# The 16-bit copy of thirteen weight rows goes from ScalarE to GpSimd, in a kernel of window attention and a two-layer product

## The chip, the cores and the metric

The kernel runs on one core of a Trainium2 chip. The metric is the device time of one execution in microseconds. Engines are named as in the profile: PE (TensorE, matrix products), DVE (VectorE), ACT (ScalarE), POOL (GpSimd) and SP (SyncE, which here starts the transfers). Each takes its own instructions in order and waits at an instruction until what it reads has been written and what it overwrites has been read.

## The reference

Attention over four batches, eight heads, 768 positions and a head size of 64, with four sink keys and a window of 128 keys; then a layer of 512 x 2048 with the square of the positive part, and one of 2048 x 512.

```python
scores = scale * np.matmul(q, k.transpose(0, 1, 3, 2))
keep = is_sink | in_window
scores = np.where(keep, scores, -1000000000.0)
scores = scores - np.max(scores, axis=-1, keepdims=True)
a = np.exp(scores)
a = a / (np.sum(a, axis=-1, keepdims=True) + 1e-09)
attn_out = np.matmul(a, v).astype(np.float32)
x = np.ascontiguousarray(attn_out.transpose(0, 2, 1, 3)).reshape(B * S, H * D)
h = np.maximum(x @ w_in, 0.0)
out = (h * h @ w_out).astype(np.float32)
```

The weights w_in and w_out come as 64-bit numbers and are turned into pairs of 32-bit ones on the chip.

## The kernel before

The tokens are taken in eight chunks of 384 (half a batch). A chunk has four pairs of heads; "pair" below is one pair of heads of one chunk, counted from the first. For a pair, PE makes scores (L255), DVE masks them out of PSUM and finds the largest (L263), ACT takes the exponential and the sums (L266), DVE makes the reciprocal of the sums (L279, L280), and POOL multiplies the probabilities by it (L291, three instructions for each of the two heads) and copies the sink part out (L304, L305). PE transposes the probabilities (L360), ACT and DVE copy them out of PSUM (L367, L365), PE multiplies them with the values (L408, L411), and ACT and DVE write the result as a high and a low part, x (L419, L420).

The products of the two layers go over 16 blocks of 128 hidden columns: PE makes ph (L467, 12 matmuls), ACT the squares (L478, L481, L483), DVE the low part gl (L490), PE adds the block into po (L505), which needs gh, gl and the block's row of w_out.

The weights come in 32 rows of 128 x 512 numbers, loaded as raw (L564). A row is made into a high and a low part by `split_steps`: DVE forms the high part t (L575, L577), a copy takes one 16-bit word of each number into one half of m (L579) while DVE puts other bits into the other half (L580), DVE takes the exponent eb (L582), ACT writes the high part to its place (L588), and DVE forms the low part from m and eb (L589), so L589 waits for the copy. The tile m has one buffer: the copy of a row waits for L589 of the row before. In the order of the rows, rows 0 to 3 are of w_in, 4 to 6 of w_out (wo), 7 to 10 of w_in (wi), 11 to 15 of w_out, 16 of w_in.

The first two chunks and rows 0 to 16 (`EARLY` is 17) stand in a part whose order is written out by hand for all five engines (L628 to L751): the instructions of each engine stand as the code calls them. `fill(n)` puts in n further steps of the rows, `normalise` the instructions of POOL for a pair. After that part a scheduler with priorities sets the order. The probabilities of a head have four buffers, the scores of this part two banks ("att") most of the time.

Of the kernel before, what the change touches and what calls it, by code (L numbers as in the profile page):

```python
# [37 lines left out]
def f32(ap):  # L38
    return ap.bitcast(F32)
# [3 lines left out]
def sink_window_attention_moe(  # L43
# [11 lines left out]
    nc = tc.nc  # L55
# [13 lines left out]
    with ExitStack() as fast:  # L69
# [490 lines left out]
        def load_row(n):  # L560
            if n in raws or n >= NROW:
                return
            raws[n] = wp.tile([P, WR, 2], I32, tag=f"wo{NFC - 4 + n % 4}", name=f"raw_{n}")
            nc.sync.dma_start(out=raws[n].rearrange("p w t -> p (w t)"), in_=row_of(n))  # L564

        def split_steps(n):
            kind, fq, j = order[n]
            load_row(n)
            top = raws[n][:, :, 1]
            words = raws[n].rearrange("p w t -> p (w t)").bitcast(U16).rearrange("p (w t) -> p w t", t=4)  # L570
            t1 = ap2.tile([P, WR], I32, tag="t1", name=f"t1_{n}")
            m = ap1.tile([P, WR], I32, tag="m", name=f"m_{n}")
            eb = ap1.tile([P, WR], I32, tag="eb", name=f"eb_{n}")
            m16 = m.bitcast(U16).rearrange("p (w t) -> p w t", t=2)
            nc.vector.tensor_scalar(t1, top, 3, 0x3FFFF000, op0=ALU.logical_shift_left, op1=ALU.bitwise_and)  # L575
            yield
            nc.vector.scalar_tensor_tensor(t1, top, -0x40000000, t1, op0=ALU.bitwise_and, op1=ALU.bitwise_or)  # L577
            yield
            nc.scalar.copy(m16[:, :, 0], words[:, :, 1])  # L579
            nc.vector.tensor_scalar(m16[:, :, 1], words[:, :, 2], 0x1FF, None, op0=ALU.bitwise_and)  # L580
            yield
            nc.vector.tensor_scalar(eb, t1, -0x800000, None, op0=ALU.bitwise_and)  # L582
            yield
            if kind == "i":
                row = wi[:, j, fq]
            else:
                row = wo[j] = wp.tile([P, 2, DM], F32R, tag=f"wo{j}", name=f"wo_{j}")
            nc.scalar.copy(row[:, 0, :], f32(t1))  # L588
            nc.vector.scalar_tensor_tensor(row[:, 1, :], m, 2.0**-36, f32(eb), op0=ALU.mult, op1=ALU.mult)  # L589
            load_row(n + AHEAD)  # L590

        def split_row(n):
            keep = tc.cur_priority
            tc.cur_priority = keep + (10 if n >= HALF else 0)
            for _ in split_steps(n):
                pass
            tc.cur_priority = keep + 12
# [19 lines left out]
        def row_steps():  # L617
            for n in range(NROW):
                yield from split_steps(n)
                split.append(n)  # L620
                yield
# [5 lines left out]
        EARLY = HALF + 1  # L627
# [396 lines left out]
```

## Time and profile before

| | |
|---|---|
| three runs, median | 701.47 us (700.86 to 702.70) |
| the profiled execution | span 701.0 us |
| PE busy | 685.4 us |
| DVE, ACT, POOL busy | 430.6, 438.5, 228.6 us |
| L579 on ACT | 32 copies, 24.8 us |

The span goes from the first to the last instruction of the profiled execution; the page has no other time for it. In the order in time, the first number of a row is the start in us and the second the duration in us (of all the instructions that the row merges, x3 for three), and what stands in brackets is idle time of the engine before it and what ended it. An instruction can start on an engine shortly before the one ahead ends. In the groups of one line, three durations in ns are the shortest, the median and the longest.

### The profile page before, as it was taken

How to read it: one execution, taken by the hardware profiler on the slowest of the kernel's cores; microseconds unless marked ns; L12 is line 12 of the kernel's file. 1: busy time of each engine (PE TensorE's matmuls, PEld its weight loads, DVE VectorE, ACT ScalarE, POOL GpSimd, SP SyncE). 2: the span in 40 equal slices, each digit the busy share in tenths (PEclk: the TensorE clock that was granted, in tenths of full speed). 3: DMA queues.
4: the chain of work that ended last, by engine and by line, in shares of the span. 5: the costliest groups of instructions: out<-in, count | busy, mean ns of one | idle time of the engine just before them, and what ended most of it. 6: DMA issues, size and time to landing. Idle time of an engine off the chain costs nothing.

```text
span 701.0 us, 11730 instructions
## 1 busy us (share of the span) xinstructions
PE 685.4 (98%) x3862; PEld 593.2 (85%) x3862; DVE 430.6 (61%) x1181; ACT 438.5 (63%) x1240; POOL 228.6 (33%) x433
## 2 busy tenths in 40 slices
PE   8889999999999999999999999999999999999995
PEld 4567889998888888888889888888988889889994
DVE  7989799746567666565565666666556665542221
ACT  6888877655666776676667777667676544422221
POOL 5764400034464432342343443233244242200000
PEclk9999999999999999999999999999999999999998
DMA  7476476412424323332434432243432210010001
GB/s 240 154 225 197 141 230 211 128 51 62 130 74 141 104 81 106 108 112 82 119 91 148 123 99 79 82 143 91 114 104 78 73 44 16 0 41 6 1 0 51
DMA packets 37028, 71.51 MB, mean 102 GB/s; under 512 B 4384, under 2 KB 14368, under 8 KB 36960
## 3 DMA queue, kind: packets, MB, share of 16 engines
q1 hardware_dynamic: 36816, 70.55, 34.1%
q8 instruction: 33, 0.54, 0.3%
q14 instruction: 35, 0.29, 0.1%
q10 hardware_dynamic: 144, 0.13, 0.1%
HBM read 62.80 MB, written 7.86 MB: 101 GB/s over the span
## 4 chain that ended last, share of the span: by engine, by line
PE 92%; ACT 3%; DVE 2%; POOL 2%; issue 1%; DMA 0%; SPq 0%; POOLq 0%; DVEq 0%
PE po L505 37%; PE ph L467 37%; PE xo L408 6%; PE s L259 5%; PE pt L378 2%; PE xo L411 2%; PE s L255 1%; POOL P L291 1%; ACT P L266 1%; PE pt L360 1%; DVE P L263 0%; DMA kn<-in_k_dram 0%; ACT m L579 0%; POOL PSK L304 0%; DVE t L577 0%
## 5 line engine op out<-in xcount | busy, mean ns | idle before, releaser
L467 PE MATMUL ph<-x,wi 128*128 128x384 f32 x1536 | 305.7, 340 | 0.0
L467 PEld LDWEIGHTS ph<-x,wi 128*128 128x128 f32 x1536 | 265.1, 188 | 9.1 <-issue 1.4
L505 PE MATMUL po<-wo,gh 128*128 128x512 f32 (+1 forms) x770 | 244.2, 398 | 0.0
L227 POOL TENSOR_TENSOR KS<-kn,KS 128x408 fp32r<-128x408 f32 (+1 forms) x48 | 58.4, 1217 | 317.0 <-ACT KS L226 317.0
L505 PEld LDWEIGHTS po<-wo,gh 128*128 128x128 f32 x770 | 135.9, 188 | 19.1 <-issue 1.3
L505 PE MATMUL po<-wo,gl 128*128 128x512 f32 x385 | 151.6, 394 | 0.0
L266 ACT ACTIVATE P<-P,nbs 128x264 f32<-128x264 f32 (+1 forms) x192 | 94.3, 491 | 75.7 <-DVE nbs L263 75.4
L486 DVE TENSOR_TENSOR ph<-ph,r 128x384 f32<-128x384 f32 x96 | 54.0, 562 | 76.7 <-ACT r L478 76.6
L263 DVE CUSTOM_DVE_ANT_0 P<-s,masks 128x264 f32<-128x264 f32 x160 | 67.1, 429 | 53.3 <-PE s L259 49.5
L291 POOL TENSOR_SCALAR P<-P,rs 128x136 f32<-128x136 f32 (+2 forms) x192 | 85.5, 461 | 30.1 <-DVE rs L280 23.4
L478 ACT ACTIVATE r<-ph 128x384 f32<-128x384 f32 x96 | 46.7, 487 | 77.7 <-PE ph L467 74.9
L490 DVE TENSOR_TENSOR gl<-ph,gh 128x384 fp32r<-128x384 f32 x128 | 71.0, 555 | 25.2 <-ACT ph L483 13.5
L505 PEld LDWEIGHTS po<-wo,gl 128*128 128x128 f32 x385 | 72.2, 188 | 16.0
L229 DVE TENSOR_TENSOR QS<-qn,QS 64x384 fp32r<-64x384 f32 x48 | 43.7, 910 | 25.0 <-ACT QS L228 24.6
L259 PE MATMUL s<-KS,QS 128*128 128x264 f32 (+1 forms) x288 | 56.9, 280 | 0.0
L286 POOL TENSOR_TENSOR P<-P 128x256 f32<-128x256 f32 (+1 forms) x48 | 48.1, 1001 | 26.7 <-ACT P L266 26.2
L259 PEld LDWEIGHTS s<-KS,QS 128*128 128x128 f32 x288 | 51.9, 188 | 5.0 <-DVE nbs L263 0.5
L481 ACT ACTIVATE gh<-r 128x384 fp32r<-128x384 f32 x96 | 50.2, 523 | 2.1
L384 DVE TENSOR_TENSOR PTF<-pt,halves 128x256 f32<-128x256 f32 x96 | 36.3, 418 | 21.8 <-PE pt L378 21.1
L408 PE MATMUL xo<-PTF,vn 128*64 128x256 f32 x448 | 45.9, 342 | 0.7 <-ACT PTF L367 0.7
L408 PEld LDWEIGHTS xo<-PTF,vn 128*64 128x64 f32 x448 | 31.2, 136 | 17.4 <-issue 9.3
L226 ACT CAST KS<-kn 128x408 fp32r<-128x408 f32 (+1 forms) x48 | 28.3, 589 | 26.0 <-issue 12.6
(108 smaller groups left out, 676.0 us busy)
## 6 DMA issues: line engine op xcount, KB each, us to landing
raw<-in_moe_w_in_dram SPq DMA_DIRECT2D x16, 512.0 KB, 4.5
raw<-in_moe_w_out_dram SPq DMA_DIRECT2D x16, 512.0 KB, 3.4
half<-in_moe_w_in_dram SPq DMA_DIRECT2D x32, 256.0 KB, 3.0
half<-in_moe_w_out_dram SPq DMA_DIRECT2D x32, 256.0 KB, 3.1
kn<-in_k_dram SPq DMA_DIRECT2D x24, 272.0 KB, 4.1
qn<-in_q_dram SPq DMA_DIRECT2D x32, 192.0 KB, 3.8
out_dram<-ob SPq DMA_DIRECT2D x23, 256.0 KB, 2.5
kn<-in_k_dram SPq DMA_DIRECT2D x24, 204.0 KB, 3.6
```

Source lines behind the costliest of these rows:

```text
L227: nc.gpsimd.tensor_tensor(KS[:, 1, 0:nk], st["kn"][:, hh, 0:nk], f32(KS[:, 0, 0:nk]), op=ALU.subtract)
L259: nc.tensor.matmul(ps[:, 0:n], st["QS", hh][:, qcols], flat[:, a, c0 : c0 + n], start=(a == 0), stop=(a == 1))
L263: nc.vector.tensor_tensor_reduce(Pt[:, i, 0:n], ps[:, 0:n], mask[:, 0:n], -SCALE, BIG, ALU.add, ALU.min, nb)
L266: nc.scalar.activation(Pt[:, i, 0:n], Pt[:, i, 0:n], AF.Exp, bias=nb, scale=-1.0, accum_out=sm[:, i : i + 1])
L286: nc.gpsimd.tensor_tensor(Pt[:, j0:NQ, 0:P], Pt[:, j0:NQ, 0:P], Pt[:, j0:NQ, BS:BAND], op=ALU.add)
L291: nc.gpsimd.tensor_scalar(Pt[:, j, 0:n], Pt[:, j, 0:n], rs[:, hh, j : j + 1], 1.0, op0=ALU.mult, op1=ALU.mult)
L408: nc.tensor.matmul(xo[h * D : h * D + D, cols], lhsT, rhs, start=(n == 0), stop=False, skip_group_check=True)
L467: nc.tensor.matmul(ph[:, 0:TOK], wi_at(i, cc, fc), xt[:, cc, :], start=(m == 0), stop=(m == 3 * NCC - 1),)
L481: nc.scalar.activation(gh, r, AF.Square)
L486: nc.vector.tensor_tensor(ph[:, 0:TOK], ph[:, 0:TOK], r, op=ALU.mult)
L490: late = lambda: nc.vector.tensor_tensor(gl, ph[:, 0:TOK], f32(gh), op=ALU.subtract)
L505: nc.tensor.matmul(po[t][:, e], gt[:, ts_], wo[f][:, i, e], start=(f == f0 and j == 0), stop=(f == f1 - 1 and j == 2), skip_group_check=True,)
```

## The change

One line. For rows 4 to 16 the copy is called on POOL (`nc.gpsimd.tensor_copy`) instead of ACT; rows 0 to 3 and 17 to 31 stay as they were.

```diff
             nc.vector.scalar_tensor_tensor(t1, top, -0x40000000, t1, op0=ALU.bitwise_and, op1=ALU.bitwise_or)
             yield
-            nc.scalar.copy(m16[:, :, 0], words[:, :, 1])
+            (nc.gpsimd.tensor_copy if 4 <= n < EARLY else nc.scalar.copy)(m16[:, :, 0], words[:, :, 1])
             nc.vector.tensor_scalar(m16[:, :, 1], words[:, :, 2], 0x1FF, None, op0=ALU.bitwise_and)
             yield
```

What this does to the order on POOL, at the end of the sixth pair's normalisation (P of pair index 1 in the second chunk; the last number of a name only tells tiles apart), with rows 6 to 9 added:

```order
 L304 CAST PSK_140<-P_1_1_642 128x6x8
 L305 TENSOR_TENSOR PSK_140<-P_1_1_642,PSK_140 128x3x8
+L579 COPY m_707<-raw_650 128x512
+L579 COPY m_757<-raw_690 128x512
+L579 COPY m_791<-raw_731 128x512
+L579 COPY m_845<-raw_788 128x512
 L291 TENSOR_SCALAR P_2_0_808<-P_2_0_808,rs_2_0_869 128x264 x3
```

Four copies now stand between two normalisations; the first is that of row 6. Further on, rows 10 to 12 stand behind the seventh pair's normalisation, around the two passes that make the low part of KS for the ninth pair:

```order
 L305 TENSOR_TENSOR PSK_139<-P_2_1_813,PSK_139 128x3x8
+L579 COPY m_888<-raw_842 128x512
+L579 COPY m_957<-raw_885 128x512
 L227 TENSOR_TENSOR KS_0_1_1682<-kn_0_1672,KS_0_1_1682 128x408
+L579 COPY m_990<-raw_936 128x512
 L227 TENSOR_TENSOR KS_0_0_1676<-kn_0_1672,KS_0_0_1676 128x408
 L291 TENSOR_SCALAR P_3_0_1006<-P_3_0_1006,rs_3_0_1057 128x264 x3
```

Row 4 stands behind the fourth pair's normalisation, row 5 behind the fifth's, and rows 13 to 16 behind the eighth's in the same manner. On DVE nothing moves; around row 6 (m_707, written out as wo_728) its order is, before and after:

```order
L490 TENSOR_TENSOR gl_0_664<-ph_0_624,gh_0_663 128x384
L279 TENSOR_SCALAR rs_1_0_693<-sm_1_636 128x6
L280 RECIPROCAL rs_1_0_693<-rs_1_0_693 128x6
L575 TENSOR_SCALAR t_6_706<-raw_650 128x512
L577 SCALAR_TENSOR_TENSOR t_6_706<-raw_650,t_6_706 128x512
L580 TENSOR_SCALAR m_707<-raw_650 128x512
L582 TENSOR_SCALAR eb_708<-t_6_706 128x512
L589 SCALAR_TENSOR_TENSOR wo_728<-m_707,eb_708 128x512
```

The reciprocal rs_1_0_693, which starts the sixth pair's normalisation on POOL, stands five instructions ahead of the L589 of row 6, which waits for a copy that stands on POOL behind that normalisation. On ACT the thirteen copies are gone. On PE one matmul of L467 and on SP one transfer of kn for the ninth pair stand a few places later.

## The prediction

> **What bounds the kernel now.** I read the page first, then busy time by stage, the chain of waits over the first 100 us, and last the order in time of each engine between 30 and 95 us, where the thirteen rows lie.
>
> ```profile
> span 701.0 us, 11730 instructions
> PE 685.4 (98%) x3862; PEld 593.2 (85%) x3862; DVE 430.6 (61%) x1181; ACT 438.5 (63%) x1240; POOL 228.6 (33%) x433
> ```
>
> TensorE (PE) is busy for 98% of the span. What delays it in the hand-ordered part is therefore paid at the end: nothing later has idle time in which to win it back. By stage (us, then PE, PEld, DVE, ACT, POOL busy):
>
> ```profile
> 40.00:50.00 10.00, 7.76 (x45) 5.81 (x44) 9.27 (x25) 9.49 (x27) 7.63 (x12) 1.00 0.86 289
> 50.00:60.00 10.00, 10.00 (x58) 7.10 (x56) 9.00 (x29) 8.17 (x22) 2.60 (x6) 1.00 0.53 171
> 80.00:90.00 10.00, 10.00 (x69) 8.70 (x68) 7.16 (x16) 7.53 (x15) 0.86 (x3) 1.00 0.44 144
> ```
>
> PE idles 2.24 us between 40 and 50; from 50 it is full. But VectorE (DVE) is 90 to 93% busy right behind it, so DVE has next to no idle time that could swallow a wait. Only at 80 to 90 us is it looser. The chain of waits shows what the copy of line 579 does on ScalarE (ACT) today:
>
> ```profile
> 43.37 0.77 ACT m L579
> 44.16 0.69 DVE wo L589
> 46.85 0.02 issue
> 46.88 0.62 ACT wo L588
> ...
> 89.49 0.79 ACT m L579
> ```
>
> The copy is on the chain twice: at 43.37 (row 5) DVE's L589 waits for it, and at 89.49 (row 16) ACT itself is late.
>
> **The change, part by part.** Thirteen copies (rows 4 to 16) leave ACT and join the queue of GpSimd (POOL). An engine takes its instructions in order, so what counts is what stands ahead of each copy on POOL, and when DVE's L589 of that row, which reads the copy, comes up.
>
> ACT first: each copy takes 0.775 us, of which about 0.65 is its share of the queue (the next instruction starts before it ends).
>
> ```profile
> L579 ACT COPY m<-raw x32: 753/775/802, 10.3 to 130.3; 128x512 uint16<-128x512 uint16 x32
> ```
>
> 13 x 0.65 = 8.4 us of ACT work go. That is worth something only where PE waits for ACT.
>
> The price of a copy on POOL. No such copy stands in the trace. Rows that bound it (a fill; a pass with one input; one with two; and the shortest, median and longest of L291 in ns):
>
> ```profile
> 3.51 0.52 POOL L162 MEMSET halves<- 128x512 f32 x1
> 37.85 1.66 POOL L291 TENSOR_SCALAR P<-P,rs 128x264 f32<-128x264 f32 x3 [4.01 <-ACT x L419]
> 72.73 1.07 POOL L227 TENSOR_TENSOR KS<-kn,KS 128x408 fp32r<-128x408 f32 x1 [5.30 <-ACT KS L226]
> ...
> L291 POOL TENSOR_SCALAR P<-P,rs x192: 362/378/1278, 11.1 to 611.8; 128x136 f32<-128x136 f32 x120, 128x264 f32<-128x264 f32 x40, 128x128 f32<-128x128 f32 x32
> ```
>
> Below, 0.52: as many elements written, none read. Above, 1.07 x 512/408 = 1.34. The nearest is L291, one input and one output: 0.55 for 264 elements. The shortest L291 of all took 0.362, which can only be one of the narrow forms, taken here as 136 wide; so about 1.45 ns an element, and 0.55 + 248 x 0.00145 = 0.9 us. I take 0.9. [...]
>
> Now where the copies stand. Between 33 and 82 us POOL does nothing but normalise the probabilities (L291, L304, L305: one head, then the other) and two KS passes. Its rows in time, with the ends that matter:
>
> ```profile
> 43.27 0.47 POOL L305 TENSOR_TENSOR PSK<-P,PSK 128x24 fp32r<-128x24 f32 x1
> 45.82 2.29 POOL L291 TENSOR_SCALAR P<-P,rs 128x264 f32<-128x264 f32 x3 [2.08 <-DVE rs L280]
> 48.17 0.56 POOL L304 CAST PSK<-P 128x48 fp32r<-128x48 f32 x1
> ...
> 49.09 2.37 POOL L291 TENSOR_SCALAR P<-P,rs 128x264 f32<-128x264 f32 x3
> 51.52 0.56 POOL L304 CAST PSK<-P 128x48 fp32r<-128x48 f32 x1
> 52.16 0.29 POOL L305 TENSOR_TENSOR PSK<-P,PSK 128x24 fp32r<-128x24 f32 x1
> 59.70 2.09 POOL L291 TENSOR_SCALAR P<-P,rs 128x264 f32<-128x264 f32 x3 [7.25 <-DVE rs L280]
> 62.77 2.68 POOL L291 TENSOR_SCALAR P<-P,rs 128x264 f32<-128x264 f32 x3
> 66.11 0.28 POOL L305 TENSOR_TENSOR PSK<-P,PSK 128x24 fp32r<-128x24 f32 x1
> 66.36 1.06 POOL L227 TENSOR_TENSOR KS<-kn,KS 128x408 fp32r<-128x408 f32 x1
> 77.04 0.22 POOL L304 CAST PSK<-P 128x48 fp32r<-128x48 f32 x1
> 77.75 2.25 POOL L291 TENSOR_SCALAR P<-P,rs 128x264 f32<-128x264 f32 x3
> ```
>
> And the instructions of DVE that read the copies, with those that PE waits for (last row: shortest, median, longest in ns):
>
> ```profile
> 47.87 0.78 DVE L589 SCALAR_TENSOR_TENSOR wo<-m,eb 128x512 fp32r<-128x512 int32 x1
> 53.00 0.43 DVE L263 CUSTOM_DVE_ANT_0 P<-s,masks 128x264 f32<-128x264 f32 x1
> 63.18 0.78 DVE L589 SCALAR_TENSOR_TENSOR wi<-m,eb 128x512 fp32r<-128x512 int32 x1
> 66.77 1.20 DVE L589 SCALAR_TENSOR_TENSOR wo<-m,eb 128x512 fp32r<-128x512 int32 x1 [0.46 <-ACT m L579]
> 72.78 1.56 DVE L589 SCALAR_TENSOR_TENSOR wo<-m,eb 128x512 fp32r<-128x512 int32 x1
> 78.16 0.78 DVE L589 SCALAR_TENSOR_TENSOR wo<-m,eb 128x512 fp32r<-128x512 int32 x1
> 79.20 0.54 DVE L490 TENSOR_TENSOR gl<-ph,gh 128x384 fp32r<-128x384 f32 x1
> 85.86 0.56 DVE L420 TENSOR_TENSOR x<-xo,x 128x384 fp32r<-128x384 f32 x1 [2.70 <-ACT x L419]
> ...
> L589 DVE SCALAR_TENSOR_TENSOR wo<-m,eb x16: 681/686/1560, 39.8 to 132.9; 128x512 fp32r<-128x512 int32 x16
> ```
>
> *Row 4* runs in POOL's idle time before 37.85: free. *Row 5* can start when the normalisation of the fifth pair ends, 43.27 + 0.47 = 43.74, and ends at 44.64; L589 began at 44.16. DVE is 0.5 us late. Behind it stand L280 (which starts the next normalisation) and the L577 for which ACT's L588 at 46.88 waits, so all three engines pass this 0.5 on.
>
> *Row 6* is the dear one. Its copy stands behind the whole normalisation of the sixth pair, which ended at 52.45, while L589 of row 6 wanted it at 47.87. DVE then stands still with everything behind it: row 7's steps, the scores' L263, the next gl. Standing still, it leaves POOL alone, and POOL goes faster: three L291 took 1.66 where they met little of DVE, 2.29 and 2.37 here; the small casts 0.22 against 0.56. From 48.1 POOL has the first head's casts (0.22 + 0.29, each after a gap of some 0.07), the second head's L291 (1.66) and its casts left, some 2.9 us: 51.0, and 51.5 with the 0.5 from row 5. The copy ends at 52.4. DVE is late by 52.4 - 47.87 = 4.5 us. Rows 7 to 9 stand directly behind on POOL and each needs only the L589 before it, so they make no wait; but rows 7 and 8 share memory time with DVE's L577, as the normalisation did before: I set 0.2 for it. DVE reaches the L263 of 53.00 late by 4.7. What PE does about it:
>
> ```profile
> 53.49 1.06 PE L255 MATMUL s<-kn,qn 64*128 64x264 f32 x4
> 68.09 0.73 PE L505 MATMUL po<-wo,gh 128*128 128x512 f32 x2
> 82.35 0.40 PE L505 MATMUL po<-wo,gl 128*128 128x512 f32 x1
> 92.13 1.57 PE L408 MATMUL xo<-PTF,vn 128*64 128x256 f32 x16 [0.66 <-ACT PTF L367]
> ```
>
> The scores at 53.49 go into the bank that the L263 of 53.00 empties until 53.43: a slack of 0.1. So PE loses **4.6 us** here.
>
> *Row 10* likewise: its copy stands behind the normalisation of the seventh pair, whose start (59.70) moves along with DVE. In the time of before, L589 wants it at 63.18. POOL then has some 1.3 of L291 and 0.6 of casts left, 65.1, and the copy ends at 66.0: DVE stands 2.9 us. Part of it comes back at row 11: L589 at 66.77 had waited 0.46 for ACT and lost another 0.5 to the KS pass of 66.36 (1.20 for what takes 0.69). Row 11 ends some 1.7 late. PE needs that row as wo at 68.09 + 0.23, and row 11 ended at 67.97: slack 0.35. PE loses **1.4 us**.
>
> *Row 13*: behind the eighth pair's normalisation, wanted at 78.16, ready at about 81.0; DVE stands 2.8 us. It was idle for 2.70 before 85.86, and the gl that is late next (79.20) would end at about 79.7 + 2.8 = 82.5; PE uses it from 82.35. PE loses **0.1 us**. Rows 14 to 16 stand right behind and cost nothing.
>
> *The gain*: at 92.13 PE waits 0.66 for an ACT chain that holds row 16's copy. Without it **-0.65 us**.
>
> Sum: 4.6 + 1.4 + 0.1 - 0.65 = +5.45 us on a span of 701.0. The median of the runs is 701.47, 0.47 above that span, so 706.9; I write **707.0**.
>
> The bounds: with a copy of 0.52 the terms are 3.8, 1.0, 0 and -0.65: 705.6. With 1.34 they are 5.5, 1.8, 0.5 and -0.65: 708.6; and if POOL does not go faster while DVE stands (a second head of 3.3 instead of 2.3 in both stalls), 2 more: 710.6.
>
> **The rivals.** *Every copy holds DVE up.* Under KS passes L589 took 1.20 and 1.56 where its usual time is 0.69: at 72.78 it lost 0.87 to a POOL instruction of 1.07. If the copies that make no wait each take 0.6 from DVE in that manner, rows 7 and 8 add 1.0 to the first term beyond what I set, rows 11 and 12 add 1.2 to the second, and DVE's idle time before 85.86 no longer suffices (1.0): 5.45 + 3.2 = 8.7, **710.2**. Against it: the L589 of 47.87, in the middle of a normalisation, took 0.78 and so lost only 0.09 to it. [...]
>
> *Only the first stall counts.* If PE's order leaves more room at 68 us than 0.35, since ACT is 0.65 a row ahead by then, the second term goes and the first shrinks to 4: 4 - 0.65 = 3.4, **704.9**.
>
> *ACT sets the pace, and the change is faster.* ACT is 9.49 of 10 busy at 40 to 50. If PE's idle time there and at 92.13 ends with ACT alone, and the wait of row 6 is hidden behind products that PE has in hand, the gain is all of 2.24 + 0.66 = 2.9: **698.6**. The point from which it decides is whether PE has 4.6 us of work at 53.49 that needs nothing of DVE. Against it speak the bank of the scores and the order of PE, which is written out. That the copies don't reach POOL is out: their rows stand there.
>
> **How the numbers follow.** My forecast 0.67 (own range 705.3 to 709.0), every copy holding DVE up 0.14, only the first stall 0.11, ACT setting the pace 0.04; the rest, 0.04, is a wait hidden so far that no difference shows. A measurement tells 0.3% here, 2.1 us: faster is below 699.4, slower above 703.6. Slower 0.91, within 0.3% 0.05, faster 0.04. The range takes in both neighbours: 704.2 to 710.6.
>
> **What would show it.** Right: L589 of row 6 waiting some 4 us for POOL's L579, those of rows 10 and 13 near 3, that of row 5 near 0.5; L579 on POOL at 0.9; PE idle between 50 and 75 us by some 6 where it had none; no 0.66 before the xo of 92. Wrong: a copy shorter than 0.5 or longer than 1.4; DVE waits that PE doesn't repeat; a lateness at 100 us that differs from the one at the end.

## The result

The changed kernel takes 709.61 us (median of 4 runs, 709.12 to 710.28), the kernel before beside it 701.49 us: 1.0109 times as long, 95% interval 1.0096 to 1.0122, or 8.1 us more. The forecast was 707.0, in a range of 704.2 to 710.6: slower, by the mechanism that was named, but 8.1 and not 5.5 us. The 2.6 us that were missing in the sum are the more instructive part.

The page after, and busy time by stage (columns as before: us, then PE, PEld, DVE, ACT, POOL busy; then the granted clock of PE, and the share and rate of the transfers):

```profile
span 708.3 us, 11736 instructions
PE 687.9 (97%) x3862; PEld 594.2 (84%) x3862; DVE 431.2 (61%) x1181; ACT 431.0 (61%) x1227; POOL 235.8 (33%) x446
...
40.00:50.00 10.00, 7.47 (x42) 5.64 (x43) 6.89 (x21) 7.92 (x23) 8.00 (x15) 1.00 0.69 234
50.00:60.00 10.00, 6.34 (x26) 4.37 (x25) 8.27 (x21) 3.88 (x11) 3.30 (x7) 0.89 0.44 137
60.00:70.00 10.00, 10.00 (x60) 7.61 (x59) 5.93 (x17) 6.27 (x18) 5.60 (x11) 0.94 0.51 161
70.00:80.00 10.00, 8.06 (x40) 5.28 (x39) 8.50 (x21) 5.35 (x16) 4.14 (x5) 1.00 0.41 130
```

PE, which was full from 50 us on, now has holes at 50 to 60 and at 70 to 80. And a column moved that the prediction did not look at: the granted clock, 0.89 and 0.94 where it had been 1.00.

The order in time of POOL, DVE and PE of the changed kernel, in that order:

```profile
43.41 0.77 POOL L579 COPY m<-raw 128x512 uint16<-128x512 uint16 x1
50.69 0.77 POOL L579 COPY m<-raw 128x512 uint16<-128x512 uint16 x1
52.25 0.91 POOL L579 COPY m<-raw 128x512 uint16<-128x512 uint16 x1 [0.79 <-DVE wo L589]
70.16 0.77 POOL L579 COPY m<-raw 128x512 uint16<-128x512 uint16 x1
```

```profile
44.20 0.69 DVE L589 SCALAR_TENSOR_TENSOR wo<-m,eb 128x512 fp32r<-128x512 int32 x1 [0.84 <-POOL m L579]
51.50 0.69 DVE L589 SCALAR_TENSOR_TENSOR wo<-m,eb 128x512 fp32r<-128x512 int32 x1 [3.69 <-POOL m L579]
52.56 1.08 DVE L577 SCALAR_TENSOR_TENSOR t<-raw,t 128x512 int32<-128x512 int32 x1
55.76 1.07 DVE L577 SCALAR_TENSOR_TENSOR t<-raw,t 128x512 int32<-128x512 int32 x1
70.96 0.69 DVE L589 SCALAR_TENSOR_TENSOR wi<-m,eb 128x512 fp32r<-128x512 int32 x1 [2.63 <-POOL m L579]
73.51 0.84 DVE L580 TENSOR_SCALAR m<-raw 128x512 uint16<-128x512 uint16 x1
74.75 0.69 DVE L589 SCALAR_TENSOR_TENSOR wo<-m,eb 128x512 fp32r<-128x512 int32 x1
88.53 0.69 DVE L589 SCALAR_TENSOR_TENSOR wo<-m,eb 128x512 fp32r<-128x512 int32 x1 [2.62 <-POOL m L579]
```

```profile
41.08 1.06 PE L255 MATMUL s<-kn,qn 64*128 64x264 f32 x4 [0.53 <-DVE nbs L263]
49.28 0.66 PE L360 MATMUL pt<-ident,P 128*128 128x128 f32 x4 [1.99 <-ACT SK L316]
57.23 1.45 PE L255 MATMUL s<-kn,qn 64*128 64x264 f32 x4 [3.66 <-DVE nbs L263]
58.60 1.22 PE L505 MATMUL po<-wo,gh 128*128 128x512 f32 x2
61.36 0.71 PE L255 MATMUL s<-kn,qn 64*128 64x264 f32 x4
75.50 0.50 PE L505 MATMUL po<-wo,gh 128*128 128x512 f32 x1 [1.19 <-DVE wo L589]
82.15 1.57 PE L408 MATMUL xo<-PTF,vn 128*64 128x256 f32 x16
91.23 1.57 PE L408 MATMUL xo<-PTF,vn 128*64 128x256 f32 x16
99.18 1.57 PE L408 MATMUL xo<-PTF,vn 128*64 128x256 f32 x16
```

The four waits are all there: L589 waits 0.84, 3.69, 2.63 and 2.62 us for a copy that POOL makes only when a normalisation is through. To see what PE makes of them, take the same instructions in the kernel before:

```profile
41.36 1.06 PE L255 MATMUL s<-kn,qn 64*128 64x264 f32 x4 [0.53 <-DVE nbs L263]
56.05 0.71 PE L255 MATMUL s<-kn,qn 64*128 64x264 f32 x4
74.29 1.56 PE L408 MATMUL xo<-PTF,vn 128*64 128x256 f32 x16
83.37 1.57 PE L408 MATMUL xo<-PTF,vn 128*64 128x256 f32 x16
```

Counted from the scores at 41 us (so that the start of the kernel, which differs from execution to execution, stays out), the changed kernel is late by 4.0 us at the scores of 57.23 (before: 53.49), by 5.6 at those of 61.36 (before: 56.05), by 8.1 at the xo of 82.15 (74.29) and still at that of 91.23 (83.37), by 7.3 at that of 99.18 (92.13), and by 7.6 at the end. So the loss comes in three pieces: 4.0 with the waits of rows 5 and 6 (0.3 of it is there at the transposes of 49.28, 49.23 before, and comes from row 5), 1.6 in the few products behind it, 2.5 with the wait of row 10. Row 13 adds nothing, and 0.8 comes back at 92 us.

The 1.6 us in the middle is no wait. Two products of po, which took 0.73 us in the kernel before, take 1.22 at 58.60. Stretches of 2 us of the changed kernel (start and end, length, PE busy, granted clock, share and rate of the transfers) show why:

```profile
56.00:58.00 2.00, 0.77 (x3) 0.94 0.39 156
58.00:60.00 2.00, 2.00 (x5) 0.50 0.52 162
60.00:62.00 2.00, 2.00 (x8) 0.70 0.27 104
```

What the three stretches lack of the full clock, 2 x (0.06 + 0.50 + 0.30) = 1.7 us, is the loss of 3.4 us at half. In stretches of half a microsecond the clock is 0.78 from 57.5 to 58, 0.81 from 61 to 61.5 and 0.50 between: half from 57.78 to 61.19. So PE runs at half its clock for 3.41 us after its wait of 3.66 us.

### The profile page after: what moved, and what is told of

It is laid out like the page before. It is cut to its first block, busy times and chain, and to the rows that moved or that the text cites. A ratio compares the mean times of both kernels' runs of the same rounds, so it can differ in the third digit from the quotient of the medians.

```text
span 708.3 us, 11736 instructions
## 1 busy us (share of the span) xinstructions
PE 687.9 (97%) x3862; PEld 594.2 (84%) x3862; DVE 431.2 (61%) x1181; ACT 431.0 (61%) x1227; POOL 235.8 (33%) x446
## 4 chain that ended last, share of the span: by engine, by line
PE 90%; DVE 3%; POOL 3%; ACT 1%; issue 1%; DMA 0%; SPq 0%; POOLq 0%; DVEq 0%
PE ph L467 37%; PE po L505 37%; PE xo L408 5%; PE s L259 5%; PE pt L378 2%; POOL P L291 2%; PE s L255 1%; PE xo L411 1%; DVE t L577 1%; DVE P L263 1%; PE pt L360 1%; ACT P L266 1%; POOL PSK L304 1%; DMA kn<-in_k_dram 0%; DVE m L580 0%
## 5 line engine op out<-in xcount | busy, mean ns | idle before, releaser
L467 PE MATMUL ph<-x,wi 128*128 128x384 f32 x1536 | 305.9, 340 | 0.0
L467 PEld LDWEIGHTS ph<-x,wi 128*128 128x128 f32 x1536 | 265.1, 188 | 9.1 <-issue 1.4
L263 DVE CUSTOM_DVE_ANT_0 P<-s,masks 128x264 f32<-128x264 f32 x160 | 67.3, 429 | 55.0 <-PE s L259 49.5
L291 POOL TENSOR_SCALAR P<-P,rs 128x136 f32<-128x136 f32 (+2 forms) x192 | 82.7, 446 | 25.6 <-DVE rs L280 18.0
L490 DVE TENSOR_TENSOR gl<-ph,gh 128x384 fp32r<-128x384 f32 x128 | 71.1, 555 | 25.4 <-ACT ph L483 14.2
```

Source lines behind the costliest of these rows:

```text
L263: nc.vector.tensor_tensor_reduce(Pt[:, i, 0:n], ps[:, 0:n], mask[:, 0:n], -SCALE, BIG, ALU.add, ALU.min, nb)
L291: nc.gpsimd.tensor_scalar(Pt[:, j, 0:n], Pt[:, j, 0:n], rs[:, hh, j : j + 1], 1.0, op0=ALU.mult, op1=ALU.mult)
L467: nc.tensor.matmul(ph[:, 0:TOK], wi_at(i, cc, fc), xt[:, cc, :], start=(m == 0), stop=(m == 3 * NCC - 1),)
L490: late = lambda: nc.vector.tensor_tensor(gl, ph[:, 0:TOK], f32(gh), op=ALU.subtract)
```

## The experiments

The theory: the place of a copy in POOL's queue makes the waits, PE repeats those of rows 6 and 10, and PE's own idling then costs it the clock. The rivals: VectorE's instructions take longer beside the copies, wherever these stand (the expectations call it memory time); or any wait of VectorE reaches PE. "Lateness" below is counted from the scores at 41 us to the xo at 92 us, or from there to the end, in the one profiled execution of each kernel; medians are compared with runs of the kernel before on the same chip, which there took 701.8 to 702.1.

### The four rows behind a normalisation, and the other nine

The edit of the kernel before, for the four (for the nine, the list is 4, 7, 8, 9, 11, 12, 14, 15, 16):

```diff
-            nc.scalar.copy(m16[:, :, 0], words[:, :, 1])
+            (nc.gpsimd.tensor_copy if n in (5, 6, 10, 13,) else nc.scalar.copy)(m16[:, :, 0], words[:, :, 1])
```

> Only rows 5, 6, 10 and 13, whose copies stand on GpSimd right behind a pair's normalisation, are copied by GpSimd; the other nine of the thirteen are back on ScalarE. If the place in the queue makes the loss, the waits of L589 stay as they are (about 0.8, 3.7, 2.6 and 2.6 us), PE still stands some 3 us at the scores of 53 us and some 1.7 at 68 to 77 us, and the time is 705.5 to 708. If the loss is the memory time that the copies take from VectorE, nine of thirteen copies are gone and the time is below 704.

> The other nine (rows 4, 7 to 9, 11, 12, 14 to 16) are copied by GpSimd, rows 5, 6, 10 and 13 by ScalarE. If the place in the queue makes the loss, no L589 waits more than 0.6 us for GpSimd, and the time is that of the kernel before to within 1.5 us: 0.7 won at the xo of 92 us, up to 1.5 lost to L577 that take 1.08 in place of 0.69. If the copies' memory time makes the loss, 704 to 707.

The four: 708.91 us, 1.0094 (1.0079 to 1.0109). The nine: 706.46 us, 1.0055 (1.0036 to 1.0073). The four nearly make the loss of all thirteen, a little above what the theory gave, and their L589 wait as in the change (0.85, 3.71, 2.64 and 2.65 us). But the nine were to cost next to nothing and cost 4.4 us. Their order in time on DVE says why:

```profile
52.00 0.69 DVE L589 SCALAR_TENSOR_TENSOR wi<-m,eb 128x512 fp32r<-128x512 int32 x1 [1.71 <-POOL m L579]
53.06 1.08 DVE L577 SCALAR_TENSOR_TENSOR t<-raw,t 128x512 int32<-128x512 int32 x1
68.23 1.06 DVE L580 TENSOR_SCALAR m<-raw 128x512 uint16<-128x512 uint16 x1
69.19 1.28 DVE L582 TENSOR_SCALAR eb<-t 128x512 int32<-128x512 int32 x1
```

With row 6 back on ACT, DVE comes to row 7 while the normalisation still runs: now row 7's copy is the first behind it, and L589 waits 1.71 (that of row 14 likewise waits 0.67, at 85.65). The expectation had taken "behind the first copy" for "free", which holds only while DVE is held up at the first one. The three other rows are the rival's: under a copy L577 takes 1.08 and not 0.69, and around row 11 L580 takes 1.06 for 0.46 beside the copy and L582 1.28 for 0.42 beside the KS pass behind it (POOL, 68.89 to 70.18). Of the nine's lateness of 3.7 at the xo of 92 us, PE idles 1.84 at the scores of 54.5 us, and 2 us later its clock falls, to 0.51 at 58 to 60 us. So this pair does not clear the rival. It shows that the loss does not add up over the rows (6.8 + 4.4 against 8.1): with all thirteen, row 7 doesn't wait, since DVE is held up at row 6 first; and each kernel has its own falls of the clock (the four have two between 41 and 92 us, at 50 and 74).

### One row at a time

The edit is the same, with `n in (6,)`, `(10,)`, `(13,)` and `(16,)`.

> Only row 6 is copied by GpSimd. By the prediction's steps L589 of row 6 waits some 3.5 us behind the sixth pair's normalisation and PE repeats 3.3 of it at the scores of 53 us; where the granted clock falls to half after PE's idling, 1.2 more. Time 704.5 to 706.5. If a wait of VectorE were hidden by what PE has in hand, 702 to 703.

> Only row 10 is copied by GpSimd. By the prediction's steps L589 of row 10 waits 2.6 to 2.9 us and PE loses 1.4 of it, since the wait and the slow L589 of row 11 give some back; the time is 702.5 to 704.5. If the copies of rows 11 and 12 were what made the second loss of the change 2.5 us, L577 and L580 of rows 11 and 12 show their usual 0.69 and 0.46 here; if the wait alone makes it, PE loses 2.5 here too.

> Only row 13 is copied by GpSimd. By the prediction's steps L589 of row 13 waits some 2.6 us and VectorE's idle time before the L420 of 86 us takes it up: 0.1 us on PE, the time that of the kernel before to within 1 us. If a VectorE wait of this size always reaches PE, 704.

> Only row 16 is copied by GpSimd, where nothing stands ahead of it. By the prediction's steps PE no longer waits 0.66 us at the xo of 92 us, nothing else moves, and the time is 0.6 us below that of the kernel before (0.1%, at the edge of what the runs can tell). If VectorE's or ScalarE's next step takes the place of the wait, no difference.

| copied by GpSimd | median, us | ratio (95%) | L589 waits, us | lateness at xo, end |
|---|---|---|---|---|
| row 6 | 707.16 | 1.0071 (1.0044 to 1.0099) | 3.70 | 4.5, 4.6 |
| row 10 | 705.80 | 1.0050 (1.0034 to 1.0067) | 2.63 | 3.3, 3.4 |
| row 13 | 702.03 | 1.0000 (0.9988 to 1.0012) | 2.64 | 0.0, -0.3 |
| row 16 | 701.98 | 0.9994 (0.9985 to 1.0002) | none | -0.8, -0.7 |

Rows 10 and 13 are the nearest to a pair: a wait of 2.6 us on the same engine costs 4.0 us in the one place and nothing in the other. "Any wait of VectorE reaches PE" falls. The wait of row 13 ends in the idle time that DVE had before 86 us:

```profile
81.89 0.69 DVE L589 SCALAR_TENSOR_TENSOR wo<-m,eb 128x512 fp32r<-128x512 int32 x1 [2.64 <-POOL m L579]
```

Rows 6 and 10 cost more than expected, 5.4 for 2.7 to 4.7 and 4.0 for 0.7 to 2.7, though for row 6 the interval (3.1 to 6.9 us) and the profile's 4.6 reach into what was expected. The first line is of DVE, the others of PE, with row 10 alone:

```profile
66.36 1.50 DVE L589 SCALAR_TENSOR_TENSOR wi<-m,eb 128x512 fp32r<-128x512 int32 x1 [2.63 <-POOL m L579]
69.63 0.50 PE L505 MATMUL po<-wo,gh 128*128 128x512 f32 x1 [0.45 <-ACT wo L588]
70.91 0.65 PE L505 MATMUL po<-wo,gh 128*128 128x512 f32 x1 [0.78 <-DVE wo L589]
71.79 1.05 PE L505 MATMUL po<-wo,gh 128*128 128x512 f32 x2
...
72.00:74.00 2.00, 2.00 (x7) 0.50 0.42 162
```

PE idles 0.45 and 0.78, and loses 0.4 more in a ph that takes 2.68 for 2.32, as it waits 0.37 for this L589: 1.6 us, close to the 1.4 of the prediction. But this is not the wait alone. With rows 11 and 12 back on ACT, the KS pass stands directly behind row 10's copy on POOL (66.25 to 67.31), and beside it L589 takes 1.50 for 0.69. Behind it the clock is 0.50, and that makes up the rest of the 3.3 us. L577 and L580 of rows 11 and 12 show 0.69 and 0.45 here. In the change they show 1.08 and 0.84, its second loss is 2.5, and the clock between 70 and 80 us is 1.00. So there it is the wait and what POOL takes from DVE in rows 11 and 12, here the wait, the KS pass and the clock.

With row 6 alone, PE idles 2.91 us at the scores of 56 us and the clock falls right behind, as in the change. PE is 3.0 us late at these scores, against 4.0 in the change. The difference agrees with the 0.3 of row 5 and the 0.4 that each L577 of rows 7 and 8 loses beside its copy, work that stands on DVE between row 6 and these scores.

Row 16's gain is in the profile, 0.8 us at the xo of 92 us, but the medians cannot tell its 0.1% from nothing.

### Filling PE's idle time

The edit adds products on PE that nothing reads, in a bank that is free there, 14 ahead of the scores of 57 us; in the second kernel also 8 ahead of the transposes of 49 us (the two lines with `s == 4` are only in the second).

```diff
+            def fillers(n):
+
+                t = bank("xo", "fill")
+                for _ in range(n):
+                    nc.tensor.matmul(t, idle[:, 0:P], idle, start=True, stop=True)
...
+                if s == 4:
+                    fillers(8)
...
-                    todo += [lambda s=s, i=i: scores(s, i) for i in range(1, NQ)]
+                    todo += [lambda s=s, i=i: (s == 6 and i == 1 and fillers(14), scores(s, i)) for i in range(1, NQ)]
```

> The change, with 14 extra products of 128x128 by 128x512 bf16 on PE (into the free bank of xo, their result unused) at the place where PE idles 3.7 us before the scores of 57 us. If the granted clock of 0.89 after that wait comes from PE's idling, the first products of po behind the scores go back from 1.22 to 0.73 us for two, the clock shows 1.00 and the time is 1.0 to 1.3 us below that of the change (708.3 to 708.6). If the clock falls for another cause, the time is that of the change, 709.6, or above.

> The change, with extra products on PE (unused, into the free bank of xo) at two places: 8 ahead of the transposes of 49 us, where PE idles 2.0 us, and 14 ahead of the scores of 57 us, where it idles 3.7. If PE's idling makes the clock fall, it stays at full between 45 and 70 us, and the time is 1.0 to 2.4 below that of the change: 707.2 to 708.6. If not, 709.6 or more.

The first took 709.77 us (707.68 to 712.53), no better than the change; the second 708.05 us (707.64 to 708.60), 1.6 below it. The ratios to the kernel before are 1.0101, 1.0086 and, for the change, 1.0109, and the intervals of the last two still overlap (1.0063 to 1.0108, 1.0096 to 1.0122), so the profiled executions have to carry the reading. In the first, the place that was filled did run at full clock, but the clock had fallen elsewhere. Its stretches of 2 us, and the products behind the filled place:

```profile
50.00:52.00 2.00, 0.86 (x6) 0.93 0.11 27
52.00:54.00 2.00, 2.00 (x7) 0.50 0.00 0
...
57.03 2.97 PE L650 MATMUL fill<-idle 128*128 128x512 bf16 x13
59.93 0.72 PE L255 MATMUL s<-kn,qn 64*128 64x264 f32 x4
60.57 0.73 PE L505 MATMUL po<-wo,gh 128*128 128x512 f32 x2
```

Behind the 2.0 us of idling at 49 us it was half for 3.4 us, and from 7 to 14 us, in the start, where the scores of 41 us came only at some 42.9 (the transposes that follow came at 51.14, and at 49.28 in the change with its scores at 41.08). Counted from them, the lateness at the xo of 92 us is 6.3, 1.0 less than that of the change. With both places filled, no stretch between 0 and 100 us of the profiled execution was below full clock, all waits of DVE were still there (0.84, 3.69, 2.63, 2.64), and the scores behind the filled place started with PE having idled 0.63:

```profile
48.79 0.66 PE L360 MATMUL pt<-ident,P 128*128 128x128 f32 x4 [0.25 <-ACT SK L316]
56.76 1.06 PE L255 MATMUL s<-kn,qn 64*128 64x264 f32 x4 [0.63 <-DVE nbs L263]
```

The lateness at the xo of 92 us is 5.8, 1.5 less than the change's 7.3. That prices the clock in the change: 1.5 of its 7.3 us, with no work saved and no wait shortened. It is one execution: in the other three the mean granted clock over the execution is 0.991 to 0.994, against 0.996 in the profiled one, which suggests that it fell there somewhere.

### The copies ahead of the normalisation

All thirteen copies stay on GpSimd, but the POOL part of the normalisations of the sixth to eighth pair is held back and put in behind a copy: the first head's behind that of row 6, 10 or 13, the second head's behind the next row's. (In the profile of this kernel the lines are some digits higher: L598 is L589, L586 is L579, L367 is L360, L323 is L316.)

```diff
-            for hh in heads:
+            def scale(heads=heads):
+                for hh in heads:
...
+            if c == 1 and p in (1, 2, 3):
+                held.extend([lambda: scale((0,)), lambda: scale((1,))])
+            else:
+                scale()
...
+            if n in (6, 10, 13, 7, 11, 14):
+                held.pop(0)()
```

> All thirteen rows are copied by GpSimd as in the change, but the normalisations of the sixth, seventh and eighth pair are put in later on GpSimd: the first head's behind the copy of row 6, 10 or 13, the second head's behind the copy of the next row. If the place in the queue makes the loss, the waits of 3.7, 2.6 and 2.6 us are gone and the time is 699.5 to 702; ScalarE's 8.4 us can then win at most the 1.3 + 0.4 + 0.7 us in which PE waited for it before. If the copies' memory time makes it, 704 or more.

702.35 us against 702.07, 1.0008 (0.9996 to 1.002): the loss is gone, with the same thirteen copies on the same engine. Of the waits only row 5's is left, and L589 of row 6 starts without one:

```profile
43.66 0.69 DVE L598 SCALAR_TENSOR_TENSOR wo<-m,eb 128x512 fp32r<-128x512 int32 x1 [0.85 <-POOL m L586]
47.67 0.78 DVE L598 SCALAR_TENSOR_TENSOR wo<-m,eb 128x512 fp32r<-128x512 int32 x1
```

This settles the place in the queue as the cause of the loss: by the rival, 704 or more was due, and DVE's work takes longer here too (L580 of row 7, L589 in this kernel, takes 1.02 at 49.45 for 0.46). But nothing is won either, though ACT is 8 us lighter. PE has one idle time of 2.3 us where it had 1.28 and 0.43, and behind it the clock is half:

```profile
49.04 1.11 PE L367 MATMUL pt<-ident,P 128*128 128x128 f32 x4 [2.30 <-ACT SK L323]
...
50.00:52.00 2.00, 2.00 (x7) 0.50 0.32 78
```

The SK copy stood on ACT behind the L588 of row 6, which waits for DVE. So a last version wrote that high part later:

```diff
-            nc.scalar.copy(row[:, 0, :], f32(t1))
+            if n == 6:
+                late_high.append(lambda: nc.scalar.copy(row[:, 0, :], f32(t1)))
+            else:
+                nc.scalar.copy(row[:, 0, :], f32(t1))
...
+            if n == 7:
+                late_high.pop()()
```

> The woven order, and in it ScalarE writes the high part of row 6 (L588) later, behind the two copies of PTF, so that the SK copy for which PE idled 2.3 us at 49 us no longer stands behind it. If that one long idling is what costs the woven order its gain (the clock fell to half for 3 us behind it), PE's wait there is below 0.8, the clock stays full, and the time is 1.0 to 1.6 below that of the woven order: 700.5 to 701.5, level with the kernel before or 0.2% below. If VectorE sets the pace of 40 to 70 us, PE waits as long a little later, at the scores, and the time is that of the woven order.

703.74 us, 1.0020 (1.0011 to 1.0029): slower than the kernel before, and of the two theories of the expectation the second fits. PE's wait moved to the scores (here L257 is L255 and L265 is L263):

```profile
54.53 1.06 PE L257 MATMUL s<-kn,qn 64*128 64x264 f32 x4 [2.81 <-DVE nbs L265]
```

Between 40 and 55 us DVE sets the pace: with the wait for ACT gone, PE waits for DVE instead, only later and in one piece. The clock stayed full behind these 2.81 us, and still nothing was won, so the fall alone is not what cost the woven order its gain. In their profiled executions both woven kernels are 0.2 late at the end, counted from 41 us; where the 1.6 us between the medians of this last kernel and the kernel before arise is not shown. No version beat both kernels by more than the runs can tell.

## Why the prediction was right, and where it was wrong

**Right: the queue.** The step "what counts is what stands ahead of each copy on POOL" holds, and so do its four places. The waits were forecast at 0.5 (on top of the 0.5 of before), 4.5, 2.9 and 2.8; L589 of row 5 came 0.3 later than before, counted from 41 us, that of row 6 3.9 later, and those of rows 10 and 13 waited 2.63 and 2.62. They are shorter in part because the copy is: 0.77 us in all four, not 0.9. In row 6 the second head's three L291 also took 1.40 where I had set 1.66. The shortest copy on POOL took 0.766 us, so my price, scaled from L291, was 0.13 too dear for a copy that DVE stands still for.

**Right: the third wait costs nothing and row 16's copy gives 0.65 back.** Row 13 alone 1.0000; 0.8 us at 92 us.

**Wrong: the sum had no term for the clock.** The step that failed is "so PE loses 4.6 us here": it took PE's loss for its lateness at the next scores. That was 4.0; but PE then ran at half its clock and lost 1.6 more on products that waited for nothing. In the page before, the clock column reads 1.00 in every quoted stage, and I read it as a constant. With PE's idle time filled at both places it stayed full in the profiled execution, so in the change it goes with PE's idling. Between 0 and 100 us the stretches of 2 us show twelve falls in these traces: the clock reads 0.50 to 0.51 in the stretches that a fall fills, and what the stretches of one fall lack of the full clock is 1.70 to 1.72 us in eleven, 3.4 us at half, and 3.42 us in one, 6.8 at half. Where one trace has several, they start whole multiples of 3.41 us apart, as far as the stretches tell: at some 26.0, 49.9 and 73.8 us in the kernel of the four, seven times each, and 44.4 us apart, thirteen times, in the first filled kernel (7.3 and 51.7) and with row 10 alone (26.7 and 71.1). No one size of idle time decides it. It came after single idle times of 1.84 (the nine), 2.0 (the first filled kernel) and 2.3 us (woven), and after 0.45 and 0.78 close together (row 10 alone and the four). It did not come after the 1.99 us at 49 us of the change, the 2.81 of the last kernel, or the 0.37, 1.19 and 0.38 of the change at 74 to 77 us. Ahead of every fall PE had idled 1.1 us or more within 5 us, but so it had where none followed; what decides between them stays open.

**Wrong: the second wait, 1.4 for 2.5.** The wait costs 1.6 with row 10 alone, the KS pass beside L589 included. The term for what the copies of rows 11 and 12 take from DVE was left out there, and I gave 0.2 for rows 7 and 8, where the two L577 lose 0.8. In the change L577 of rows 7, 8, 11 and 12 takes 1.08 for 0.69 beside a copy, and L580 of row 11 takes 0.84 under the KS pass that follows the copy. The rival "every copy holds DVE up" had it right that DVE loses time beside a copy, and put it too high (0.6 a copy for 0.4), and as the main cause it falls with the woven order. How much it loses goes with how long the two run together: L577 at 52.56 starts with 0.60 us of the copy left and loses 0.39, and one at 89.94 with 0.25 left takes 0.73 and loses 0.04, so in these two the loss is what is left of the copy less some 0.2. Why DVE loses it is not shown.

**The forecast of 707.0 came as near as it did by errors that partly cancel:** the first wait 0.6 too dear, the clock 1.6 and the second wait 1.1 too cheap. The measured 709.6 lies above my own range (705.3 to 709.0) and inside the stated one, and that is luck: its upper end stood for a copy of 1.34 us and a POOL that gets no faster while DVE stands, and neither was so. The 710.2 of the rival "every copy holds DVE up" is nearer, and just as much by chance. From 41 us to the end the profiled executions differ by 7.6 us, the medians by 8.1; single executions of the kernel before lie up to 1.8 us apart, so the 0.5 between the two says nothing.

## What to carry to other kernels

An instruction that goes to a less busy engine takes the place in that engine's queue that the program order gives it (here row 6's copy came at 50.69, behind the normalisation, and its reader waited 3.69 us): look up what stands ahead of it and when its reader comes, before its duration or the relief of the old engine. The same 2.6 us of waiting cost 4.0 us (the fall of the clock behind it included) or nothing, by what the reader's engine had behind it. When PE is made to idle, put the slow clock after it into the range as well: here it came after some idle times and not after others of the same size, and 3.4 us at half the clock are an estimated loss of up to 1.7 us each time.

## What the hardware showed that was not expected

- The granted clock fell to 0.50 for some 3.4 us at a time, once for 6.8, after PE had idled for as little as 1.1 us in all (row 10 alone, between 22 and 26 us), and stayed full after 2.81 us in one piece (the last kernel); the price in the change was 1.5 us. Where it falls differs between kernels, also in the first 30 us, where PE idles in the kernel before as well.
- A copy of 128x512 16-bit words, every fourth word read and every second written, takes POOL 0.77 us in five of the change's thirteen rows, the four that DVE waits for among them, as long as ACT takes for it (0.775). In the other eight it takes 0.89 to 0.92, and up to 0.97 in the kernel of the nine.
- The start of the kernel up to the scores of 41 us differed by 2.4 us between profiled executions (40.53 to some 42.9) whose instructions up to there differ only in which engine makes row 4's copy; a median of several runs is needed for less than that.
